# Squared-ReLU attention and a low-rank mixer on one core: the first eight outputs of batch 0 built in another order

## The chip, the cores and the metric

The kernel runs on one core of one Trainium2 chip. The metric is the device time of one execution in microseconds (us). Its engines: PE (TensorE, matmuls; PEld is its weight load), ACT (ScalarE), DVE (VectorE), POOL (GpSimd, which here issues the casting DMAs), SP (SyncE, which here issues the transposing DMAs).

## The reference

```python
# u, v: 8 x 3136 x 256; z: 8 x 3136 x 64; float32
scores = (1.0 / S) * np.matmul(z, z.transpose(0, 2, 1))
attn = np.maximum(scores, 0.0) ** 2
x = u * np.matmul(attn, v)
# U: 3136 x 32, V: 32 x 3136, w_ch1: 256 x 1024, w_ch2: 1024 x 256
h = x.transpose(0, 2, 1) @ U @ V
m = x + h.transpose(0, 2, 1)
out = m + np.maximum(m @ w_ch1, 0.0) @ w_ch2
```

Scores are symmetric in the two positions. The inputs have no bias and no mask.

## The kernel before, in words

The 3136 rows are 24 full tiles of 128 and a tail of 64, 25 in all (NT), of which tile 24 (NF) holds the tail twice over two halves of partitions. A *block* (o, j) is the 128x128 piece of attn that joins output tile o to tile j of v. By symmetry only about half of the blocks are computed: the *panel* `A[j]` holds the 13 blocks (j+k, j), k from 0 to 12, indices modulo 25. `score` (L272) makes pieces of panels: two matmuls on two halves of the array into one tile `ps2` of two PSUM banks (`pair_psum`; there are two such tiles), a ReLU with scale on ACT (L291), a square on DVE (L293). `score_steps` (L295) cuts a panel into two pieces of 832 columns. The other blocks of an output o are those of `A[o]` transposed: `turn` (L311) has SP issue one transposing DMA of 12 blocks into a *strip* (five buffers).

An output's accumulation (`half`, L351) is 49 matmuls, each block against v in two halves of 64 rows that run side by side. Two neighbouring outputs share two PSUM banks (`sets`, two of them); `close_pair` (L360) copies and adds the halves and multiplies by u. The main loop goes over the outputs in the order 12, 13, ..., 24, 0, ..., 11 and has as filler the scores that later outputs need, by hand-written tables (`first_at`, `own_at`, `next_at`). From batch 1 on, the mixer of the batch before (`rank`, `mix`, `low_rank`, and the two channel matmuls L520 and L562, in *bursts*) runs between the outputs.

The engines' order is the program's own. Each engine has one queue, and so have the DMAs of POOL and of SP: an instruction that waits holds those behind it.

Batch 0 has no earlier batch in which its scores could be made ahead. So `start_up` (L607) makes its first eight outputs in two groups of four:

- z comes by POOL DMAs that cast to bf16 (`load_z`, L174), is doubled to 128 columns on DVE (`double_z`, L188), and turned on PE against a unit matrix (`turn_on_pe`, L204), with copies on ACT and DVE (L212).
- Group 1, outputs 12 to 15: for all 25 tiles j the 512 columns of these outputs are scored, in pairs of j. For j from 3 to 11 they are places in `A[j]`; for the other 16 tiles they go to scratch in batch 1's v buffer and in `x_bf`, so that v of batch 1 can only be loaded later. The pair i is scored while the pair i-2 is used. The panels 16 to 19 are made from the middle of this group on, in `nxt`.
- At the border the two pairs close, batch 1's z is doubled (`double_z`) and turned whole by one SP DMA, w2 is fetched (`fetches[3]`).
- Group 2, outputs 16 to 19: stored scores for j from 4 to 15, strips for the rest, with panels 20 to 23 and the rest of panels 8 to 15 (`rest`, 128 to 1024 columns wide) between.

Then the main loop begins with output 20 (i = 8), and loads v of batch 1 in nine pieces at i from 9 to 23.

Of the kernel before, what the change touches and what calls it, by code (L numbers as in the profile page):

```python
# [7 lines left out]
FP32 = mybir.dt.float32  # L8
# [34 lines left out]
def kernel(  # L43
# [11 lines left out]
    nc = tc.nc  # L55
# [136 lines left out]
    def turn_z(b, parts):  # L192
        z_bf = z_tiles[b]
        for t0, t1 in parts:
            transpose(
                out=zT_of(b)[:, t0 : upto(t1), :],
                in_=z_bf[:, t0 : upto(t1), :, :].rearrange("p t h c -> p (t h c)"),
            )
    def turn_on_pe(parts, banks):

        z_bf = z_tiles[0]
        for (t0, t1), ps in zip(parts, banks):
            for t in range(t0, t1):
                mm(  # L204
                    out=ps[:, (t - t0) * P : (t - t0 + 1) * P],
                    lhsT=z_bf[:, t, :, :].rearrange("p h c -> p (h c)"),
                    rhs=eye,
                    start=True,
                    stop=True,
                )  # L210
            copy = nc.vector.tensor_copy if t0 % 8 else nc.scalar.copy
            copy(  # L212
                out=zT_first[:, t0:t1, :].rearrange("p t c -> p (t c)"),
                in_=ps[:, : (t1 - t0) * P],
            )
# [17 lines left out]
    def weight_steps():  # L233
# [21 lines left out]
        def copies():  # L255
# [4 lines left out]
            lambda: wide(w1_bf, moe_w_ch1),  # L260
            narrow,
            fetch,
            lambda: wide(w2_bf, moe_w_ch2),
        ]
        third = FIRST // 2
        puts = [lambda t=t: put(t, t + third) for t in range(0, NF, third)]
# [338 lines left out]
            begun.add((t0, h))  # L605

    def start_up():  # L607
        parts = ((8, 16), (0, 8), (16, NF))
        load_z(0, parts[:2])
        nc.gpsimd.memset(eye, 1.0)  # L610
        nc.gpsimd.affine_select(
            out=eye,
            in_=eye,
            pattern=[[1, P]],
            base=0,
            channel_multiplier=-1,
            compare_op=ALU.is_equal,
            fill=0.0,
        )
        load_v(0, (8, 12))  # L620
        load_v(0, (12, 18))
        load_z(0, parts[2:])
        for part in [(3, 8), (0, 3), (18, NF), (NF, NT)]:
            load_v(0, part)
        double_z(0, parts[:2])
        turn_on_pe([(8, 12), (12, 16)], sets[0])
        turn_on_pe([(0, 4), (4, 8)], sets[1])
        nc.gpsimd.memset(U_bf[:, NF, :], 0.0)
        outs = [FIRST + i for i in range(NG)]
        c0 = FIRST * P  # L630
        for o in outs[::2]:
            open_pair(0, o)
            load_u(0, o)
        if B > 1:
            load_z(1, WHOLE)
        for s in fetches[:3]:
            s()
        nxt = [s for j in range(LEAD, LEAD + NG) for s in turned(0, j)]
        rooms = [v_both[1][:, t : t + 4, :] for t in range(0, NF, 4)]
        rooms = [r.rearrange("p (a t) d -> p a (t d)", a=2) for r in rooms]  # L640
        rooms += [x_bf[:, g].rearrange("p (a w) -> p a w", a=2) for g in (2, 3)]
        pairs = [(8, 9), (10, 11), (12, 13), (14, 15), (6, 7), (3, 4), (5,), (1, 2)]
        pairs += [(0, 16), (17, 18), (19, 20), (21, 22), (23, 24)]
        where = {}

        def make(pair):
            if all(LEAD - 1 - HALF <= j < FIRST for j in pair):
                todo = []
                for j in pair:
                    at = (FIRST - j) * P  # L650
                    where[j] = A[j][:, at : at + NG * P]
                    todo.append((j, c0, NG * P, where[j]))
                score(0, todo)
            else:
                room = rooms.pop(0)
                for i, j in enumerate(pair):
                    where[j] = room[:, i, :]
                score(0, [(j, c0, NG * P, room) for j in pair])

        seen = []  # L660

        def use(pair):
            for j in pair:
                for o in outs:
                    at = (o - FIRST) * P
                    stop = [o % 2 == 1 and len(seen) == NT - 1 - h for h in range(2)]
                    beside(o, j, where[j][:, at : at + P], stop)
                seen.append(j)

        for i, pair in enumerate(pairs):  # L670
            if i == 3:
                double_z(0, parts[2:])
            if i == 5:
                ps = pair_psum()
                turn_on_pe([(16, 20), (20, NF)], [ps[:, 0, :], ps[:, 1, :]])
                turn_on_pe([(NF, NT)], [pair_psum()[:, 0, :]])
                extend_z(0)
            make(pair)
            if i > 5 and i % 2:
                nxt.pop(0)()  # L680
            if i > 1:
                use(pairs[i - 2])
        for pair in pairs[-2:]:
            nxt.pop(0)()
            use(pair)
        for o in outs[1::2]:
            close_pair(0, o)

        outs = [LEAD + i for i in range(NG)]
        for o in outs[::2]:  # L690
            open_pair(0, o)
            load_u(0, o)
        fetches[3]()
        if B > 1:
            double_z(1, WHOLE)
            turn_z(1, WHOLE)
        pairs = [(j, j - 1) for j in range(LEAD - 1, LEAD - FIRST, -2)]

        def use_stored(js):
            for j in js:  # L700
                for o in outs:
                    if 0 <= o - j <= HALF:
                        beside(o, j, block(0, o, j))

        def make_stored(pair):
            todo = []
            for j in pair:
                k0, k1 = LEAD - j, min(NB, LEAD + NG - j)
                todo.append((j, LEAD * P, (k1 - k0) * P, A[j][:, k0 * P : k1 * P]))
            score(0, todo)  # L710

        nxt += [lambda pair=pair: make_stored(pair) for pair in pairs[:2]]
        own = [lambda j=j: use_stored([j]) for j in outs]
        for s in _merge(nxt, own):
            s()
        rest = []
        for j in range(FIRST - NG, LEAD):
            rest += score_steps(0, j, LEAD + NG - j, NB)
        more = [s for j in range(LEAD + NG, LEAD + 2 * NG) for s in score_steps(0, j)]
        for i, pair in enumerate(pairs):  # L720
            if i + 2 < len(pairs):
                make_stored(pairs[i + 2])
            else:
                more.pop(0)()
            use_stored(pair)
            if i == len(pairs) - 1:
                turn(0, LEAD + NG)
        tail = []
        for o in outs:
            js = [(o + 1 + i) % NT for i in range(HALF)]  # L730

            def close(o=o, j=js[-1]):
                beside(o, j, block(0, o, j), [o % 2 == 1] * 2)
                if o % 2:
                    close_pair(0, o)
                if o == outs[1]:
                    load_u(0, LEAD + NG)
                if o < outs[-1]:
                    turn(0, o + NG + 1)

            for i in range(3):
                some = js[4 * i : min(4 * i + 4, HALF - 1)]
                tail.append(lambda o=o, js=some: [beside(o, j, block(0, o, j)) for j in js])
            tail.append(close)
        for s in _merge(tail, more + rest):
            s()

# [3 lines left out]
    for j, i in enumerate((6, 7, 8, 9, 3, 5, 4, 2, 9, 8, 7, 6)):  # L753
        own_at[i].append((j, 0, FIRST - j))

    first_at = {8: [(NT - 1, 0, NB), (0, 0, NB)], 9: [(1, 0, NB)], 10: [(2, 0, NB)]}
    first_at.update({11: [], 12: []})
    for j, i in zip(range(3, FIRST), (9, 10, 11, 11, 11, 12, 12, 12, 12)):
        first_at[i].append((j, 0, FIRST - j))

    next_at = {i: [] for i in range(NT)}
    for j in range(FIRST):
# [12 lines left out]
    for b in range(B):  # L775
# [2 lines left out]
        bursts = bursts_of(b - 1) if b else []  # L778
        burst_at = {4: (0, 1), 8: (2, 3), 13: (4, 5), 17: (6, 7)}
        own = own_at if b else first_at  # L780
        v_at = dict(zip((9, 11, 12, 14, 16, 18, 20, 22, 23), V_PARTS)) if b == 0 else {}
        ahead = dict(zip((2, 3, 6, 7, 10, 11, 14), range(NC)))
        for i in range(begin, NT):
            o = turns(i)
            fill = [s for key in own.get(i, ()) for s in score_steps(b, *key)]
            if more:
# [4 lines left out]
                    turn_z(b + 1, ((FIRST, NF),))  # L791
                if b and i == 10:
                    turn_z(b + 1, ((0, FIRST),))
                if i == 11:
                    extend_z(b + 1)
                if i in v_at:
                    load_v(b + 1, v_at[i])
            main = attend_steps(b, o)
            if b and i in ahead:
                main.insert(17 if (i + (i > FIRST)) % 2 == 0 else 10, lambda c=ahead[i]: low_rank(b - 1, c))  # L800
            _spread(main, fill)
            if i + AHEAD < NT:
                turn(b, turns(i + AHEAD))
            elif more:
                turn(b + 1, turns(i + AHEAD - NT))
            elif i == NT - AHEAD:
                turn_x(b, 0)
            if b == 0 and i in puts:
                puts[i]()
            if b and i == 0:  # L810
# [64 lines left out]
```

## Time and profile before

| what | value |
|---|---|
| four runs, median | 1015.03 us |
| the four | 1013.11, 1025.04, 1014.01, 1016.04 us |
| profiled execution: its own time | 1013.11 us |
| its span, first to last instruction | 1011.4 us |
| TensorE clock granted | 1.00 |
| ACT busy | 613.1 us (61%) |
| DVE busy | 541.3 us (54%) |
| POOL busy | 172.2 us (17%) |
| ReLUs of scores (L291), squares (L293) | 469, 469 |
| strips, issue to landing, median of 196 | 5.3 us |
| u loads of 256 KB, issue to landing, median of 96 | 3.8 us |

How to read it: a group's line gives source line, engine, operation, out<-in, and count; then busy time, mean duration of one, and the idle time of the engine before it with what ended it. In the chain of waits each piece has its start, its length and what it was: work of an engine, or a DMA that something waited for. In a timeline the bracket holds the engine's idle time before and its releaser. A duration is an instruction's own; when like instructions follow one another they overlap, and the spacing is shorter than the duration.

### The profile page before, as it was taken

How to read it: one execution, taken by the hardware profiler on the slowest of the kernel's cores; microseconds unless marked ns; L12 is line 12 of the kernel's file. 1: busy time of each engine (PE TensorE's matmuls, PEld its weight loads, DVE VectorE, ACT ScalarE, POOL GpSimd, SP SyncE). 2: the span in 40 equal slices, each digit the busy share in tenths (PEclk: the TensorE clock that was granted, in tenths of full speed). 3: DMA queues.
4: the chain of work that ended last, by engine and by line, in shares of the span. 5: the costliest groups of instructions: out<-in, count | busy, mean ns of one | idle time of the engine just before them, and what ended most of it. 6: DMA issues, size and time to landing. Idle time of an engine off the chain costs nothing.

```text
span 1011.4 us, 31331 instructions
## 1 busy us (share of the span) xinstructions
PE 988.8 (98%) x13856; PEld 782.3 (77%) x13856; DVE 541.3 (54%) x977; ACT 613.1 (61%) x834; POOL 172.2 (17%) x318
## 2 busy tenths in 40 slices
PE   7799999999999999999999999999999999999998
PEld 5578777787778877788787887878877788777856
DVE  5878654456544664446644556445664356542242
ACT  7877664666645776456764667556674666643154
POOL 4122112121121211121112211112112120011000
PEclk9999999999999999999999999999999999999999
DMA  9999979999898998989989987989979998767432
GB/s 171 148 197 225 179 151 195 179 176 152 163 199 164 177 169 170 166 181 170 159 176 166 183 168 144 193 173 188 156 155 195 170 184 143 144 137 173 101 97 97
DMA packets 414584, 167.70 MB, mean 166 GB/s; under 512 B 389408, under 2 KB 399328, under 8 KB 414448
## 3 DMA queue, kind: packets, MB, share of 16 engines
q1 hardware_dynamic: 384944, 99.16, 60.0%
q0 software_dynamic: 29504, 66.55, 28.0%
q8 instruction: 108, 1.77, 0.7%
q14 instruction: 28, 0.23, 0.1%
HBM read 61.88 MB, written 25.69 MB: 87 GB/s over the span
## 4 chain that ended last, share of the span: by engine, by line
PE 90%; DVE 4%; DMA 3%; ACT 2%; issue 1%; DVEq 0%; ACTq 0%; POOLq 0%
PE ps L351 46%; PE ps L562 17%; PE ps L520 17%; PE ps L278 6%; DMA strip<-A 1%; PE ps L385 1%; PE ps L442 1%; DVE A L293 1%; DVE x_bf L502 1%; ACT A L291 1%; PE ps L488 1%; DMA zT<-z_bf 1%; DVE both L366 1%; DVE x_bf L375 0%; ACT v L291 0%
## 5 line engine op out<-in xcount | busy, mean ns | idle before, releaser
L291 ACT ACTIVATE A<-ps 128x832 bf16<-128x832 f32 (+8 forms) x469 | 352.4, 763 | 155.9 <-PE ps L278 147.1
L351 PE MATMUL ps<-v,A 64*128 64x256 bf16 x4864 | 333.3, 269 | 4.9 <-DVE A L293 2.8
L293 DVE TENSOR_TENSOR A<-A 128x832 bf16<-128x832 bf16 (+8 forms) x469 | 240.5, 524 | 147.3 <-ACT A L291 143.5
L351 PE MATMUL ps<-v,strip 64*128 64x256 bf16 x4420 | 307.3, 269 | 2.5 <-DMA strip<-A 2.5
L351 PEld LDWEIGHTS <-A 64*128 64x128 bf16 x4864 | 238.5, 94 | 48.4 <-issue 13.1
L538 ACT ACTIVATE relu_bf<-ps 128x1024 bf16<-128x1024 f32 (+2 forms) x208 | 187.7, 908 | 142.3 <-PE ps L520 140.3
L351 PEld LDWEIGHTS <-strip 64*128 64x128 bf16 x4420 | 221.7, 94 | 37.2 <-DMA strip<-A 3.0
L562 PE MATMUL ps<-w_bf,relu_bf 128*128 128x256 bf16 x1600 | 204.8, 273 | 0.2 <-ACT relu_bf L536 0.2
L573 DVE TENSOR_TENSOR o_sb<-ps,x_bf 128x512 f32<-128x512 f32 (+1 forms) x104 | 69.7, 670 | 247.4 <-PE ps L562 231.9
L520 PE MATMUL ps<-ut,w_bf 128*128 128x512 bf16 (+2 forms) x896 | 199.4, 353 | 0.3 <-ACT relu_bf L538 0.3
L562 PEld LDWEIGHTS <-relu_bf 128*128 128x128 bf16 x1600 | 155.9, 98 | 47.3 <-issue 3.2
L335 POOL DMA_DIRECT2D u_sb<-in_u_dram x96 | 53.6, 559 | 468.5 <-DVE x_bf L375 435.5
L520 PEld LDWEIGHTS <-w_bf 128*128 128x128 bf16 x896 | 85.0, 98 | 61.1 <-issue 7.0
L278 PE MATMUL ps<-zT 64*128 64x416 bf16 (+8 forms) x812 | 130.7, 312 | 0.0
L365 ACT COPY both<-ps 128x512 f32<-128x512 f32 (+1 forms) x104 | 58.8, 567 | 73.1 <-PE ps L351 65.4
L581 POOL DMA_DIRECT2D out_dram<-o_sb x84 | 46.0, 548 | 270.8 <-DVE o_sb L573 266.8
L366 DVE TENSOR_TENSOR both<-ps,both 128x512 f32<-128x512 f32 (+1 forms) x104 | 69.3, 666 | 27.3 <-ACT both L365 26.9
L375 DVE TENSOR_TENSOR x_bf<-both,u_sb 128x512 bf16<-128x512 f32 (+1 forms) x104 | 69.8, 671 | 3.6
L502 DVE TENSOR_TENSOR x_bf<-ps,x_bf 128x512 bf16<-128x512 f32 (+1 forms) x112 | 65.4, 626 | 8.1 <-PE ps L488 8.0
L278 PEld LDWEIGHTS <-zT 64*128 64x128 bf16 x812 | 42.2, 94 | 4.0
L225 POOL DMA_DIRECT2D v<-in_v_dram x61 | 34.4, 567 | 0.2 <-PE ps L520 0.2
L278 PE MATMUL ps<-relu_bf 64*128 64x416 bf16 (+9 forms) x121 | 23.1, 339 | 2.4 <-ACT A L291 1.3
(52 smaller groups left out, 230.2 us busy)
## 6 DMA issues: line engine op xcount, KB each, us to landing
u_sb<-in_u_dram POOLq DMA_DIRECT2D x96, 256.0 KB, 3.8
out_dram<-o_sb POOLq DMA_DIRECT2D x84, 256.0 KB, 3.0
v<-in_v_dram POOLq DMA_DIRECT2D x57, 192.0 KB, 4.3
strip<-A SPq DMA_TRANSPOSE x196, 5.3
out_dram<-o_sb SPq DMA_DIRECT2D x12, 256.0 KB, 2.1
z_c<-in_z_dram POOLq DMA_DIRECT2D x7, 384.0 KB, 6.3
w_bf<-in_moe_w_ch_dram POOLq DMA_DIRECT2D x2, 512.0 KB, 8.0
u_sb<-in_u_dram POOLq DMA_DIRECT2D x16, 64.0 KB, 2.7
```

Source lines behind the costliest of these rows:

```text
L278: mm(out=ps[:, k, :n], lhsT=zT[halves[k], j, :], rhs=zT_flat[halves[k], c : c + n], start=True, stop=True,)
L291: nc.scalar.activation(out=dst, in_=src, func=AF.Relu, scale=sc)
L293: nc.vector.tensor_tensor(out=dst, in0=dst, in1=dst, op=ALU.mult)
L351: mm(out=acc[t0][h][:, (o - t0) * D : (o - t0 + 1) * D], lhsT=w[halves[h]], rhs=v_both[b % 2][halves[h], j, :], start=start, stop=stop, **kw,)
L365: nc.scalar.copy(out=both[:, :w], in_=banks[1][:, :w])
L366: nc.vector.tensor_tensor(out=both[:, :w], in0=banks[0][:, :w], in1=both[:, :w], op=ALU.add)
L375: nc.vector.tensor_tensor(out=x_at(b, t0, n), in0=split(both[:, :w]), in1=u_sb[:, :n, :].rearrange("p t (a c) -> p t a c", c=P), op=ALU.mult,)
L502: nc.vector.tensor_tensor(out=q, in0=split(ps[h][:, : len(ks) * D]), in1=q, op=ALU.add)
L520: mm(out=ps[i][:, :w] if apart else ps[:, i, :w], lhsT=w1_bf[:, db, (hp + i) * P : (hp + i + 1) * P], rhs=uT[c][:, db, len(chunks[c]) * P ...
L538: nc.scalar.activation(out=relus[c][:, hp : hp + 2, :w], in_=ps[:, :, :w], func=AF.Relu)
L562: mm(out=ps[:, k * D : (k + 1) * D], lhsT=relus[c][:, ht, q : q + P], rhs=w2_bf[:, ht, :], start=(ht == 0), stop=(ht == NH - 1),)
L573: nc.vector.tensor_tensor(out=o_sb[:p, :nk, :].rearrange("p t (a c) -> p t a c", c=P), in0=split(ps[:p, : nk * D]), in1=x_at(b, t, nk)[:p] ...
```

## The change

- z's first two parts come as fp32 by SP DMAs into the two u buffers; DVE writes one copy to bf16, ACT the other (`first_z`). Seven matmuls on zeros run before. The part 16 to 24 of z is loaded and doubled as before, at an earlier place in POOL's queue, and turned before the third step.
- Group 1 makes no scratch scores. Stored scores stay, now for j from 0 to 11 as far as they lie in panels; the panels 12 to 15 are made whole, then 16 and 17. The blocks of outputs 12 to 15 on the other side of the diagonal are turned on PE against the unit matrix, 48 of them, into a `ps2` tile and copied into strips (`mirror`): two copies of 1024 columns on DVE, two of 1024 and four of 512 on ACT.
- v of batch 1: seven of nine pieces are issued by POOL right behind the fetches of w1, U and V; the last two at i = 13 and 17. A small SP read (`mark`) of the seventh piece stands in SP's queue before the first strip.
- Group 2 makes panels 18 to 22; panels 23 and 24 go to i = 8 and 9 of the main loop with their turns. Batch 1's z is doubled and turned in two parts inside group 2.
- w2 is fetched in two halves in batch 1, at i = 0 and 2.

```diff
+    def first_z(parts):
+        z_bf = z_tiles[0] = stage.tile([P, NT, 2, dqk], BF16, name="z_bf")
+        wide = zT_rest[:, :4, :].rearrange("p t c -> p (t c)")
+        nc.vector.memset(wide, 0.0)
+        ps = pair_psum()
+        for _ in range(7):
+            mm(out=ps[:, 0, :], lhsT=zT_rest[:, 0, :], rhs=wide, start=True, stop=True)
+        landed = []
+        for t0, t1 in parts:
+            z_f = u_pool.tile([P, 2, D], FP32, name="u_sb").rearrange("p a c -> p (a c)")
...
+            nc.sync.dma_start(out=z_f, in_=rows(z[0])[:, t0:t1, :])
...
+        for (t0, t1), z_f in zip(parts, landed):
+            nc.vector.tensor_copy(out=z_bf[:, t0:t1, 0, :], in_=z_f)
+            nc.scalar.copy(out=z_bf[:, t0:t1, 1, :], in_=z_f)
...
-            copy = nc.vector.tensor_copy if t0 % 8 else nc.scalar.copy
+            copy = nc.vector.tensor_copy if t0 % 8 and t1 < NF else nc.scalar.copy
...
-            lambda: wide(w2_bf, moe_w_ch2),
+            lambda: wide(w2_bf[:, NH // 2 :, :], moe_w_ch2[H // 2 :, :]),
+            lambda: wide(w2_bf[:, : NH // 2, :], moe_w_ch2[: H // 2, :]),
...
     def start_up():
-        parts = ((8, 16), (0, 8), (16, NF))
-        load_z(0, parts[:2])
+        first_z(((8, 16), (0, 8)))
...
+        load_z(0, ((16, NF),))
+        for part in [(8, 12), (12, 18), (3, 8), (18, NF), (0, 3), (NF, NT)]:
             load_v(0, part)
...
+        run(fetches[:3])
+        if B > 1:
+            for part in V_PARTS[:7]:
+                load_v(1, part)
+        turn_on_pe([(8, 12), (12, 16)], sets[0])
+        turn_on_pe([(0, 4), (4, 8)], sets[1])
+        double_z(0, ((16, NF),))
...
+        def mirror(copy, *blocks):
+            def make():
+                flat = pair_psum().rearrange("p a w -> p (a w)")
+                c = 0
+                for o, m0, m1 in blocks:
+                    for m in range(m0, m1):
+                        mm(
+                            out=flat[:, c + (m - m0) * P : c + (m - m0 + 1) * P],
+                            lhsT=A[o][:, (m + 1) * P : (m + 2) * P],
+                            rhs=eye,
...
+                    copy(
+                        out=strips[0, o][:, m0:m1, :].rearrange("p m c -> p (m c)"),
+                        in_=flat[:, c : c + n],
+                    )
...
+        steps = [
+            stored((8, 9), first), stored((10, 11), first),
+            panel(12, 0), panel(12, 1), stored((6, 7), first),
+            panel(13, 0), panel(13, 1), stored((3, 4), first),
+            mirror(by_dve, (12, 0, 8)), panel(14, 0),
+            mirror(by_act, (13, 0, 8)), panel(14, 1),
+            stored((5, 2), first), stored((1, 0), first), panel(15, 0),
+            mirror(by_act, (12, 8, 12), (13, 8, 12)), panel(15, 1),
+            mirror(by_dve, (14, 0, 8)), panel(16, 0),
+            mirror(by_act, (15, 0, 8)), panel(16, 1),
+            mirror(by_act, (14, 8, 12), (15, 8, 12)),
+            panel(17, 0), panel(17, 1),
+        ]
+        for n, (make, uses) in enumerate(steps):
+            if n == 2:
+                turn_on_pe([(16, 20), (20, NF), (NF, NT)], [*sets[1], sets[0][0]])
+            if n == 4:
+                extend_z(0)
+            if n == 18 and B > 1:
+                nc.sync.dma_start(out=mark, in_=v_both[1][:1, V_PARTS[6][1] - 1, :8])
+            make()
+            if n > 1:
+                av(steps[n - 2][1], ends)
...
+        todo = [stored(js, LEAD) for js in ((11, 10), (9, 8), (7, 6), (5, 4))]
+        rest = [s for j in range(8, FIRST) for s in score_steps(0, j, LEAD + NG - j, NB)]
+        steps = [
+            (panel(18, 0)[0], []),
+            (panel(18, 1)[0], [(o, j) for j in sides for o in low]),
+            (panel(19, 0)[0], [(o, j) for j in sides for o in high]),
+            (panel(19, 1)[0], own[16] + own[17]),
+            (todo[0][0], []),
+            (todo[1][0], own[18] + own[19]),
+            (todo[2][0], todo[0][1]),
+            (todo[3][0], todo[1][1]),
+            (panel(20, 0)[0], todo[2][1]),
+            (panel(20, 1)[0], todo[3][1]),
+        ]
+        for k, s in enumerate(rest):
+            steps.append((s, mirrored[16][3 * k : 3 * k + 3]))
+        for k in range(4):
+            steps.append((panel(21 + k // 2, k % 2)[0], mirrored[17][3 * k : 3 * k + 3]))
+        for o in high:
+            steps.append((None, mirrored[o]))
...
+            if B > 1 and n in (10, 12):
+                part = ((0, FIRST), (FIRST, NF))[n // 2 - 5]
+                double_z(1, (part,))
+                turn_z(1, (part,))
...
-    first_at = {8: [(NT - 1, 0, NB), (0, 0, NB)], 9: [(1, 0, NB)], 10: [(2, 0, NB)]}
+    first_at = {8: [(NT - 2, 0, NB)], 9: [(NT - 1, 0, NB)], 10: [], 11: [], 12: []}
+    first_turns = {8: (NT - 2,), 9: (NT - 1, 0)}
...
-        v_at = dict(zip((9, 11, 12, 14, 16, 18, 20, 22, 23), V_PARTS)) if b == 0 else {}
+        v_at = dict(zip((13, 17), V_PARTS[7:]))
...
+            if b == 1 and i in (0, 2):
+                fetches.pop()()
```

`av(uses, ends)` issues the accumulating matmuls of the listed blocks (o, j) and closes a pair behind its last one. `uses` of a step are the blocks that it makes ready; in group 1 they are accumulated two steps later, in group 2 those listed beside a step follow it at once.

## The prediction, made before the changed kernel ran

> **What bounds the kernel now.** I read the shares on the page first, then a table of windows, then the chain of waits in order of time up to 75 us, then the timeline of the same stretch.
>
> ```profile
> PE 988.8 (98%) x13856; PEld 782.3 (77%) x13856; DVE 541.3 (54%) x977; ACT 613.1 (61%) x834; POOL 172.2 (17%) x318
> ```
>
> TensorE is busy for 98% of the span. The windows say where the other 2% lies (columns: length, then busy time and instructions of PE, PEld, DVE, ACT, POOL, then clock, DMA share, GB/s):
>
> ```profile
> 0.00:60.00 60.00, 44.40 (x637) 34.37 (x639) 41.87 (x82) 46.85 (x72) 16.04 (x34) 1.00 1.02 166
> 60.00:1011.40 951.40, 944.38 (x13223) 747.97 (x13217) 499.45 (x896) 566.29 (x763) 156.11 (x284) 1.00 0.88 166
> 7.50:49.00 41.50, 33.66 (x486) 25.76 (x485) 32.33 (x64) 35.87 (x57) 8.78 (x16) 1.00 1.07 176
> 49.00:60.00 11.00, 8.29 (x139) 6.70 (x135) 7.17 (x14) 8.53 (x13) 1.07 (x2) 1.00 1.12 184
> ```
>
> In the first 60 us PE idles 60.00 - 44.40 = 15.6 us; in the other 951 us, 7.0. The change rewrites the first 49 us, so what it can win lies in those 15.6: about 5 before the first turn, 7.8 while ACT is busy for 35.87 of 41.5 us (86%), and 2.7 from 49 to 60. The chain names the waits:
>
> ```profile
> 1.30 3.04 DMA z_c<-in_z_dram
> 4.36 0.65 DVE z_bf L188 x2
> 5.06 1.89 PE ps L204 x16
> 7.53 2.06 ACT A L291 x4
> 9.59 0.93 ACT v L291
> 17.75 0.76 ACT A L291
> 29.71 1.87 DVE z_bf L188 x2
> 46.23 9.23 DMA strip<-A
> ```
>
> z's load, then ScalarE, then the doubling of z for batch 1 (1.87 us on DVE, at the border between the two groups of four), then a strip that waits for the SP queue. In the timeline:
>
> ```profile
> 13.34 0.44 PE L204 MATMUL ps<-eye,z_bf 128*128 128x128 bf16 x5 [0.67 <-ACT relu_bf L212]
> 31.61 8.56 SPq L195 DMA_TRANSPOSE zT<-z_bf  x1
> 51.11 0.72 PE L351 MATMUL ps<-v,A 64*128 64x256 bf16 x10 [1.19 <-DVE A L293]
> 55.51 0.28 PE L351 MATMUL ps<-v,strip 64*128 64x256 bf16 x1 [1.52 <-DMA strip<-A]
> ```
>
> One transpose of all of batch 1's z holds the SP queue for 8.56 us, and strips queue behind it: PE pays 1.52 us at 55.5, and 1.19 at 51.1 for a late square. The loop from output 20 on begins at 48.9 us.
>
> **The change, part by part.** Unit prices on ACT are spacings in runs of the same kind: 0.515 us for 128x512 (four in 2.06), 0.93 for 128x1024, 0.76 for 128x832; for 384, 256 and 128 columns the single durations 0.53, 0.43, 0.36 less the 0.1 by which a 512 alone (0.61) exceeds its spacing; a plain copy of 512 is 0.585.
>
> *First z.* Before, z lands at 4.33 and the first score starts at 6.88. After, SP loads it. The nearest row is SP's store of 256 KB, 2.0 us to landing (most 3.7); the POOL load took 3.0. From 0.75 that is 2.8 to 4.5; I take 3.4, the second part 0.6 later. Doubling: one copy on DVE (0.34 to 0.69) beside one on ACT (0.585), so 4.0 and 4.6. Sixteen turns at 0.09 (0.44 for five) follow, to 5.8; the first score starts at 5.85, its activation at 6.3 instead of 7.53. Gain 1.2 us, between 0 and 2. The seven matmuls on zeros lie in PE's 5 idle us and cost nothing unless they run past 4.0.
>
> *ScalarE's list up to output 20.* Before: scratch scores 8 x 0.93 = 7.44, panels 16 to 22 14 x 0.76 = 10.6, upper blocks 128 to 1024 wide 4.5, stored scores of the first group 9 x 0.515 = 4.64 and of the second 4.64 + 0.95 (384, 256 and 128 wide) = 5.6, tail turn and closes 2.1: 34.9, and the window measured 35.87. After, first group: stored 4.64 + 0.95 = 5.6, turn copies 1.43, panels 12 to 17 12 x 0.76 = 9.1, mirrored copies 2 x 0.93 + 4 x 0.585 = 4.2, a close 0.6: 20.9. Second group: panels 18 to 22 7.6, stored 5 x 0.515 + 0.95 = 3.5, rest 1.5, a close 0.6: 13.2. Together 34.1. So the scratch goes, but full panels and copies take its place: ACT saves under 1 us.
>
> *PE's list.* Score columns fall by 6912, two matmuls at a time: 3456 columns, at 0.22 us for 512, 1.5 us less. The 48 turns add 48 x 0.09 = 4.3 (bounds: half that if weight loads hide, 48 x 0.279, a turn's own duration, if nothing overlaps). PE is not the bound here, so they cost only where ACT waits.
>
> *Where the loop begins.* At ACT's share of before, 34.1 / 0.864 = 39.5 us from 6.3 is 45.8; then 24 uses of strips with no ACT work, 24 x 0.109 = 2.6 (16 matmuls in 0.87): 48.4. Bounds: ACT never waiting, 6.3 + 34.1 + 2.6 = 43.0. From above, a walk through the steps by hand: two score tiles, so a step's matmuls wait until the step two before is read out. ACT then waits 0.6 for the bank of the tail turn, 1.5 at the first mirrored block (DVE's copy of 1024 from PSUM, twice its 0.69 for 512, holds the tile), 0.9 at the third, 0.4 at several others; the first group ends at 32.0 and the loop begins at 49.3, or 50.7 if the tail of z lands at 8 and not 6.5 and holds DVE's queue, where the squares stand behind it. I take 48.4, 0.5 before today's 48.9: it rests on this stretch's own measured share.
>
> *Moved behind the loop's begin.* Panel 23, two halves, PE-bound there: 2 x 0.175 = 0.35 more.
>
> *Batch 1's z.* Doubled in two parts inside the second group, where PE uses strips and needs no square at once, and turned in halves. Halves on SP later in this trace take 1.9 to issue and 4.4 to land (median of 12), not 8.56 and 12.1. Two from 42.5 leave SP at 46.5; strip 21 lands at about 51 and is needed at the end of output 20, about 52. Output 20's blocks are all squared before. So both waits of 49 to 60 go: -2.7; 0 of it if strip 21 is 3 us late.
>
> *Loads.* Nine v pieces stood in POOL's queue behind u loads from 53 to 98 us; seven now stand behind V's fetch and ahead of the u loads of outputs 16 and 18, which are needed at 40 or later. POOL needs 0.55 each, 3.9 us, hidden. The new small SP read waits for the seventh, with strips 16 and 17 behind it; strip 16 is used from 41. Five v pieces, 1536 KB, landed between 3.04 and 15.0, 128 KB/us; seven make 1344 KB, 10.5 us, from about 23 (V landed at 24 before): 33.5, and strip 16 (3.7 to 5.5 to land) by 39: hidden. w2's halves are issued near 108 and 116 behind u's waits; at w2's own 6.8 to 9.2 us to land the second is there by 125, and the first down matmul stands at 127.25: hidden by 2 us, else it costs what is missing.
>
> A single turn in this trace has a mean duration of 279 ns, and yet five came in 0.44 us, 0.09 apart; the sum goes by the spacing. A rule of the Trainium skill speaks against this change: *TensorE: Matmul & The Clock Gate*, Part 4 (PE-mode transpose), gives about 275 ns for a 128x128 turn in a kernel's context; taken as a rate, 48 turns would be an estimated 13.2 us of PE, 8.9 more than in the sum.
>
> **Sum.** -0.5 + 0.35 - 2.7 = -2.85 on the profiled execution's 1013.1 (span 1011.4 and 1.7 around it): 1010.3. Of the four runs (median 1015.03) one, 1025.04, stands 9 us apart; the middle of the other three is 1014.0, 0.9 above the profiled one. So 1011.2.
>
> **Rivals.**
> - *ScalarE never waits.* For it: ACT had 86% already, and the new order has no border between the groups. Against: two score tiles, shared with mirrored blocks that DVE empties. The loop begins at 43.0: 5.4 less than in the sum, 1005.8.
> - *The small SP read is late: slower than before.* If the v pieces land as slowly as w2's 512 KB did (9.2 us), seven take 24, from 23 to 47; strip 16 lands at 52, PE waits 11 at 41: 1011.2 + 11 = 1022. It decides from the point where the read ends after 36. For it: DMA share 1.0 to 1.2 in this stretch. Against: v's own rate, and strips and w2 no longer run beside it.
> - *Turning costs what it saves.* The walk's 50.7 and strip 21 still late: +2.3 and +2.7: 1016. For it: DVE's PSUM copies and PE's turns stand in the same two tiles. Against: no border wait is left.
> - *Nothing of what it says is felt*: v and w2 loads cost PE no wait in the trace of before, so if the rest balances out the time is that of before, 1014.0; the sum already holds 0 for them.
>
> **How the numbers follow.** The likeliest (0.5) gives 1009 to 1014, number 1011.2. ScalarE never waiting 0.17 (1005 to 1008); turning costs what it saves 0.2 (1014 to 1018); the SP read or w2 late 0.1 (1016 to 1025); the rest, a start that gains nothing or a transfer that stalls later, 0.03. From 1005 to 1018 leaves out about 0.12. A measurement can tell about 1% (10 us) from no change. Faster by that needs 10 of the 15.6 idle us, 5 of which are the first load: 0.04. Slower by that needs the second rival at its worst: 0.05. Within 1%: 0.91.
>
> **What would show it.** Right: first score activation near 6.3; ACT busy 85 to 90% from there to the first matmul of output 20, at 47 to 49.5; no wait for a strip before 60; PE idle in the first 60 us 7 to 9 (15.6 less 2.85 less the 2.8 us of added work, less the 3 us of matmuls on zeros); the SP read over by 36; no wait at the first down matmul. Wrong: ACT waiting for PE or for a score tile at each mirrored block (loop past 50.5); the read past 36 and PE waiting for strip 16; turns spaced 0.2 us or more; loop begun before 45.

## The result, and the profile after

| what | before | after |
|---|---|---|
| median (runs) | 1016.23 us (56) | 1018.82 us (35) |
| lowest to highest | 1011.65 to 1036.77 | 1013.68 to 1026.03 |
| ratio to before, 95% interval | | 1.0022 [1.0007, 1.0037] |
| profiled execution, its span | 1013.11, 1011.4 us | 1024.6, 1022.9 us |

The change made the kernel 0.2% slower, where 0.3% faster was predicted: 1018.82 us against 1011.2. Runs of one kernel spread over more than 1%, and the two profiled executions stand on opposite sides of their medians, so their distance of 11.5 us is not the change's size; the trace shows where time goes, the ratio how much on average.

The changed kernel's lines: L207 matmuls on zeros, L223 and L231 turns of z and their copies, L298 scores, L311 ReLU, L333 strips, L195 batch 1's z, L371 accumulation, L385 and L391 a pair's close, L685 and L698 mirrored blocks and their copies, L753 the small SP read. Windows of the changed kernel, in the columns of the table before (busy time of PE, PEld, DVE, ACT, POOL, then clock, DMA share, GB/s):

```profile
0.00:60.00 60.00, 43.48 (x605) 32.99 (x607) 35.19 (x72) 42.35 (x68) 17.14 (x37) 0.97 1.06 170
60.00:1022.90 962.90, 952.88 (x13301) 757.47 (x13297) 501.88 (x902) 570.53 (x770) 153.80 (x280) 1.00 0.89 164
6.30:47.40 41.10, 34.82 (x518) 27.43 (x518) 29.30 (x62) 34.91 (x58) 10.58 (x21) 1.00 1.09 182
47.40:60.00 12.60, 3.96 (x66) 3.27 (x62) 3.50 (x6) 3.85 (x5) 1.07 (x2) 0.84 1.15 151
```

The stretch that the change rewrites is in order: from the first score to the loop's begin, ACT is busy for 34.91 of 41.1 us, 85%. But in the 12.6 us behind it PE works for 3.96. The chain of waits, some of its pieces:

```profile
1.26 3.17 PE ps L207 x7
4.43 0.68 PE ps L223 x8
6.31 1.35 ACT A L311 x3
...
38.58 7.57 DMA strip<-A
...
48.87 10.81 DMA strip<-A
...
73.76 8.41 DMA strip<-A
```

The front is as meant: z turned from 4.43, the first score activation at 6.31. Then three strips, two of them with waits of PE of over 2 us behind them. PE's timeline from the loop's begin:

```profile
47.41 0.70 PE L371 MATMUL ps<-v,A 64*128 64x256 bf16 x8
...
50.49 0.59 PE L371 MATMUL ps<-v,strip 64*128 64x256 bf16 x5
59.72 0.39 PE L371 MATMUL ps<-v,strip 64*128 64x256 bf16 x1 [8.64 <-DMA strip<-A]
...
82.80 0.35 PE L298 MATMUL ps<-zT 64*128 64x416 bf16 x2 [2.08 <-ACT A L311]
```

Output 20's first matmul starts at 47.41, 1.6 us sooner than before (48.98). Then one strip costs 8.64 us where the trace of before had 1.19, for a late square, and 1.52, for a strip. SP's timeline says which one:

```profile
30.21 0.80 SPq L753 DMA_DIRECT2D mark<-v  x1
31.06 13.09 SPq L333 DMA_TRANSPOSE strip<-A  x5
44.25 4.44 SPq L195 DMA_TRANSPOSE zT<-z_bf  x2
48.87 8.55 SPq L333 DMA_TRANSPOSE strip<-A  x2
```

Strips 16 to 20, the two halves of batch 1's z, then strip 21, issued at 48.87 and landing 10.81 us later. PE asks for a block of it at 51.1, in output 20's last step.

The first mixer matmul of batch 0 stands at 118.97 us, before at 107.94: 11.0 of the 11.5 us between the two spans are lost by then, and from there each batch takes 122.2 to 123.4 us, the last 111.1, in both kernels. Of these 11.0: the loop's begin -1.6, panel 23 +0.35 as priced, the wait for strip 21 +5.9 (8.64 less 2.71), waits between 73 and 83 +2.6 (0.54 and 2.08, none of them before), and PE work at half the clock in 59.7 to 62.8 and 83.3 to 86.7, half of which is lost, +3.2. That makes 10.5.

### The profile page after: what moved, and what is told of

The parts are those of the page before. It is cut to its first block, busy times and chain, and to the rows that moved or that the text cites. A ratio compares the mean times of both kernels' runs of the same rounds, so it can differ in the third digit from the quotient of the medians.

```text
span 1022.9 us, 31437 instructions
## 1 busy us (share of the span) xinstructions
PE 996.4 (97%) x13902; PEld 790.5 (77%) x13902; DVE 537.1 (53%) x974; ACT 612.9 (60%) x838; POOL 170.9 (17%) x317
## 4 chain that ended last, share of the span: by engine, by line
PE 89%; DMA 4%; DVE 4%; ACT 3%; issue 0%; ACTq 0%
PE ps L371 45%; PE ps L582 17%; PE ps L540 16%; PE ps L298 6%; DMA strip<-A 3%; ACT A L311 2%; PE ps L462 1%; DVE x_bf L522 1%; DVE A L313 1%; PE ps L405 1%; DMA zT<-z_bf 1%; PE ps L508 1%; DMA ut<-x_bf 1%; DVE both L386 1%; DVE x_bf L395 0%
## 5 line engine op out<-in xcount | busy, mean ns | idle before, releaser
L311 ACT ACTIVATE A<-ps 128x832 bf16<-128x832 f32 (+9 forms) x472 | 353.7, 761 | 166.1 <-PE ps L298 153.4
L371 PE MATMUL ps<-v,A 64*128 64x256 bf16 x4896 | 338.0, 271 | 0.3 <-ACT relu_bf L231 0.3
L313 DVE TENSOR_TENSOR A<-A 128x832 bf16<-128x832 bf16 (+9 forms) x472 | 241.1, 523 | 164.6 <-ACT A L311 161.3
L371 PE MATMUL ps<-v,strip 64*128 64x256 bf16 x4512 | 313.5, 269 | 9.4 <-DMA strip<-A 9.4
L371 PEld LDWEIGHTS <-A 64*128 64x128 bf16 x4896 | 243.7, 94 | 42.9 <-issue 11.2
L371 PEld LDWEIGHTS <-strip 64*128 64x128 bf16 x4512 | 228.0, 94 | 43.6 <-DMA strip<-A 10.2
L298 PE MATMUL ps<-zT 64*128 64x416 bf16 (+8 forms) x812 | 131.5, 313 | 2.1 <-ACT A L311 2.1
L385 ACT COPY both<-ps 128x512 f32<-128x512 f32 (+1 forms) x104 | 58.9, 566 | 76.1 <-PE ps L371 67.4
L386 DVE TENSOR_TENSOR both<-ps,both 128x512 f32<-128x512 f32 (+1 forms) x104 | 69.2, 666 | 28.6 <-ACT both L385 28.3
L298 PEld LDWEIGHTS <-zT 64*128 64x128 bf16 x812 | 42.9, 94 | 6.0 <-issue 2.3
L298 PE MATMUL ps<-relu_bf 64*128 64x416 bf16 (+10 forms) x112 | 21.1, 323 | 4.1 <-ACT A L311 2.4
```

Source lines behind the costliest of these rows:

```text
L298: mm(out=ps[:, k, :n], lhsT=zT[halves[k], j, :], rhs=zT_flat[halves[k], c : c + n], start=True, stop=True,)
L311: nc.scalar.activation(out=dst, in_=src, func=AF.Relu, scale=sc)
L313: nc.vector.tensor_tensor(out=dst, in0=dst, in1=dst, op=ALU.mult)
L371: mm(out=acc[t0][h][:, (o - t0) * D : (o - t0 + 1) * D], lhsT=w[halves[h]], rhs=v_both[b % 2][halves[h], j, :], start=start, stop=stop, **kw,)
L385: nc.scalar.copy(out=both[:, :w], in_=banks[1][:, :w])
L386: nc.vector.tensor_tensor(out=both[:, :w], in0=banks[0][:, :w], in1=both[:, :w], op=ALU.add)
```

## The experiments

My first theory was that batch 1's z stands in SP's queue ahead of strip 21 and takes its lead. Its rivals: the u loads of outputs 16 to 20, the small SP read, or v of batch 1 slow the strips down. All diffs are against the changed kernel unless the text says otherwise, and most runs have 12 timed executions. "Ratio" is to the kernel before, with its 95% interval. In the recorded expectations e1 and e2 are the first two experiments here, e13 and e14 the two in which batch 1's z is turned sooner; the *lead* of a strip is the time from its issue to its first use.

**Batch 1's z turned later**, in the main loop: the first half behind strip 23, the second behind strips 24 and 0.

```diff
                 double_z(1, (part,))
-                turn_z(1, (part,))
...
+            if b == 0 and i in (8, 9):
+                turn_z(1, (((0, FIRST), (FIRST, NF))[i - 8],))
```

> Changed kernel, but the two transposes of batch 1's z are issued behind strip 23 and behind strips 24 and 0 instead of ahead of strips 21 and 22. Theory Q (SP's queue of transposes is the bound between 31 and 62 us, about 3 us for each of twelve blocks, and PE waits for strip 21 because two halves of z stand before it): strip 21 lands 5 to 8 us earlier than in the changed kernel (59.6 in its profile), PE's wait of 8.6 us at 51 falls to 0 to 3, TensorE's clock stays at 1.00, and the time falls by 4 to 8 us against the changed kernel (ratio to before about 0.996). Theory U (u loads beside the transposes slow them, the order does not matter): strip 21 gains 3 at most, the wait is 5 or more, ratio 1.000 or above.

1015.72 us, ratio 0.9995 [0.9964, 1.0025], above the 0.996 that was expected. The wait near 50 is gone: strip 21 is issued at 44.13 and lands at 47.86. In 50 to 60 PE is busy throughout, against 1.36 us in the changed kernel (first row this run, second row, in a fence of its own, the changed kernel):

```profile
50.00:60.00 10.00, 10.00 (x174) 9.36 (x172) 6.82 (x14) 8.27 (x12) 1.04 (x2) 1.00 1.25 187
```

```profile
50.00:60.00 10.00, 1.36 (x22) 0.94 (x18) 1.88 (x4) 1.60 (x3) 0.54 (x1) 0.80 1.20 143
```

A wait of 1.75 us is left at 68, for strip 1, and ACT waits there too. ACT's timeline:

```profile
69.79 0.38 ACT L311 ACTIVATE A<-ps 128x256 bf16<-128x256 f32 x1 [4.17 <-DMA strip<-A]
```

ACT may not write batch 1's scores into a panel of which batch 0's strip is still being made. The same wait stands at 82.26 in the changed kernel (4.32 us). The prediction did not look at it.

**The u loads moved away**: those of outputs 16 to 19 ahead of v into other buffers, that of output 20 to group 2's start.

```diff
+        for o in (LEAD, LEAD + 2):
+            load_u(0, o, out_pool, "o_sb")
...
-            load_u(0, o)
+        load_u(0, LEAD + NG)
...
-            if n == len(steps) - 3:
-                load_u(0, LEAD + NG)
```

> Changed kernel, order of transposes kept, but u of outputs 16 to 19 is loaded ahead of batch 1's v pieces (into the output buffers, idle in batch 0), and u of outputs 20 and 21 behind those pieces; so no u load is issued between about 34 and 52 us. Theory U: the packets of a transpose take 20 to 29 ns and not 47 to 62, strip 21 lands before 53, PE's wait at 51 is 0 to 2 us, ratio to before about 0.996. Theory Q: strip 21 stays 5 us or more late, ratio 1.000 to 1.003.

1018.76 us, ratio 1.0012 [0.9983, 1.0041]. PE still waits 3.79 us for strip 21, between what the two theories expected. So these loads are not what puts strip 21 behind its use. That they lengthen the wait is possible, not shown: variants that keep them have waits of 2.01 to 8.64 us.

**Both moves together.**

> The changed kernel with the moves of e1 and of e2 together. If both theories hold in part, PE waits nowhere for a strip before 70 us, the loop's output 20 begins near 47.4 as in the changed kernel, and the time is 4 to 6 us under that of before (ratio 0.994 to 0.996), which is the sum that was predicted. If neither holds, it stays at 1.000 to 1.003.

1016.74 us, ratio 1.0024 [0.9998, 1.0049]: no wait near 50 again, and 2.38 us at 71.5. It is 1.0 us above the first experiment by the median and 2.9 by the ratio, and the intervals overlap; the 0.994 to 0.996 expected is not reached. Inconclusive on the sum, clear on the wait.

**The small SP read left out.**

```diff
-                nc.sync.dma_start(out=mark, in_=v_both[1][:1, V_PARTS[6][1] - 1, :8])
```

> Changed kernel without the small SP read of batch 1's v that stands before the first strip. In the changed kernel's profile that read is issued at 30.2 and strip 16 at 31.1, and panel 16 is not squared before about 30: theories Q and U both say no change, 0.998 to 1.002 against the changed kernel. Rival M (the read holds the strips back): strip 16 is issued 2 us or more earlier and the wait at 51 falls by as much.

1018.04 us, ratio 1.0018 [0.9988, 1.0047]; strip 21 is issued at 47.90 and PE waits 3.21 us. The read is not the cause.

**v of batch 1 loaded in the main loop** as before, and no small read.

```diff
-            for part in V_PARTS[:7]:
-                load_v(1, part)
...
-        v_at = dict(zip((13, 17), V_PARTS[7:]))
+        v_at = dict(zip((9, 11, 12, 14, 16, 18, 20, 22, 23), V_PARTS)) if b == 0 else {}
```

> Changed kernel with batch 1's v loaded in nine pieces in the main loop, as in the kernel before, and without the small SP read. Theory Q: v was not what PE waited for, early or late; strip 21 is as late as in the changed kernel without the read (PE waits 3 us at 50), and pieces beside the strips of 53 to 98 us cost 0 to 3 us more: ratio to before 1.001 to 1.005. Rival V (the early v pieces slow the start): the loop begins 1 us or more earlier than 47 and the time falls below the changed kernel's.

1020.73 us, ratio 1.0031 [1.0002, 1.006]; waits of 2.01 us at 50.4 and 3.52 at 59. Early v is not the cause.

**In the kernel before, batch 1's z turned in halves in the main loop**: the same edit as the first experiment's, with the whole turn at the border taken away.

> Kernel before with one edit: the transpose of batch 1's z leaves the border of the two groups and is issued in two halves in the main loop, behind strips 24 and 0. Theory Q (the place in SP's queue decides): strips 18 to 21 no longer stand behind it, the wait of 1.5 us for a strip at 54 goes and the one of 1.0 at 44 too; 1 to 2.5 us less than before, ratio 0.998. If the order of the queue does not matter, both waits stay and the ratio is 1.000.

1019.4 us, ratio 1.0012 [0.9981, 1.0043]. No strip wait, but now z's second half is late:

```profile
71.25 0.21 PE L278 MATMUL ps<-zT 64*128 64x64 bf16 x2 [2.79 <-DMA zT<-z_bf]
```

So z's place does not help in every order.

**Strips and halves one output further ahead**: panel 1 at i = 9, strips 1 to 4 issued an output sooner, z's halves at i = 8 and 10.

```diff
-    first_turns = {8: (NT - 2,), 9: (NT - 1, 0)}
+    first_turns = {8: (NT - 2,), 9: (NT - 1, 0, 1), 10: (2,), 11: (3,), 12: (4,)}
...
+            if b == 0 and i in (8, 10):
+                turn_z(1, (((0, FIRST), (FIRST, NF))[i // 2 - 4],))
```

> Changed kernel with the halves of batch 1's z behind strip 23 and behind strip 2, and with panel 1 scored one output earlier, so that strips 1 to 4 are issued one output earlier than in the changed kernel. e1 had a wait of 1.75 us at 68 left, and ScalarE waited 4 to 5 us to write a panel that a strip's transpose was still reading. Theory Q: both go, PE waits for no strip before 106 us, the mixer of batch 0 begins at 104 to 105 us (107.9 before, 106.2 in e1), ratio to before 0.996. Rival: the loop is bound by transposes as such, then the wait only moves, and the ratio stays at 0.999 to 1.002.

1022.4 us, ratio 1.0051 [1.0025, 1.0078]. This test failed by its own doing: z's second half, at i = 10, was begun by SP only at 65.19, behind strip 2, and was wanted at 65.8.

```profile
72.42 0.24 PE L298 MATMUL ps<-zT 64*128 64x64 bf16 x2 [6.58 <-DMA zT<-z_bf]
```

**DVE's two mirrored copies given to ACT** (`by_dve` to `by_act` for outputs 12 and 14).

> Changed kernel with the two mirrored copies that DVE made given to ScalarE, so that ScalarE makes all. By the walk of the prediction DVE's copy of 1024 columns (2 x 0.69) holds a score tile and ScalarE waits 1.5 us there: the wait goes, but ScalarE has 1.9 us more to do, so the second close of group two comes within 1 us of 47.7. If ScalarE is the bound outright, it comes 1.9 us later.

One execution, 1015.76 us. The second group's second close starts at 46.1, in the changed kernel at 47.7 and in the other variants whose first pair closes by 25.2 at 46.6 to 48.3. So ScalarE, given more work, is not later, and the wait for the strip is still 2.46. One execution does not tell a gain of 1 us.

Up to here a second theory was open: that SP's transposes are simply too many between 31 us, where the small read lets them begin, and 51, and that z is only the last of them.

**Strips 16 and 17 turned on PE**, so that SP has two transposes less; z's halves stay in group 2.

```diff
+                if part and j in (16, 17):
+                    strips[0, j] = strip_pool.tile([P, HALF, P], BF16, name="strip")
...
+            (mirror(by_dve, (16, 0, 8))[0], []),
+            (mirror(by_act, (17, 0, 8))[0], []),
+            (mirror(by_act, (16, 8, 12), (17, 8, 12))[0], []),
```

> Changed kernel with strips 16 and 17 also turned on PE, in the second group (24 turns more, one copy of 1024 columns on DVE, one on ScalarE, two of 512 on ScalarE), so that SP's transposes begin with strip 18. Theory Q2 (transposing on the DMA engines is the bound from where SP starts, 31 us, until the backlog is gone near 70; a strip costs 2.5 to 3 us of it): two strips less, so strip 21 lands 4 to 6 us earlier in respect of the loop; the loop begins 1.5 to 2.5 us later, PE's wait at 50 is 0 to 1, time 0 to 3 us under the changed kernel's, ratio to before 0.999 to 1.002. If the wait has another cause than the backlog (the u loads, the place of z), it stays at 3 us or more and the ratio goes to 1.004.

1023.32 us, ratio 1.0062 [1.0032, 1.0093]. SP has nothing to issue from 39.8 to 45.9 us, and still:

```profile
59.51 0.39 PE L371 MATMUL ps<-v,strip 64*128 64x256 bf16 x1 [4.32 <-DMA strip<-A]
```

SP's timeline of this run:

```profile
48.55 3.39 SPq L195 DMA_TRANSPOSE zT<-z_bf  x2
52.05 3.25 SPq L333 DMA_TRANSPOSE strip<-A  x1
```

The second theory falls: with room in the queue, strip 21 is again late by what stands directly before it, and it takes 7.4 us from its issue to its landing. The turns on PE cost more than they give (group 2's second close starts at 51.8, in the changed kernel's two profiles at 47.7 and 48.3).

**z late and only strip 16 on PE.**

> e1 (halves of batch 1's z behind strips 23 and 0) with strip 16 also turned on PE. Q2: the backlog that was left in e1 (a wait of 1.75 us at 68, ScalarE's wait of 4 for strip 1) is shorter by one strip; loop begins 1 us later than in e1, the mixer of batch 0 begins at 105.5 to 106.5 us (106.2 in e1), ratio to before 0.998 to 1.000. If the waits of e1 are not of the backlog, both stay and the time is 1 us over e1.

1020.26 us, ratio 1.0035 [1.0003, 1.0067]; no strip wait near 50, waits of 2.41 and 2.02 for ACT in 73 to 81.

**In the kernel before, a small SP read at the border ahead of strips 16 and 17.**

```diff
+            nc.sync.dma_start(out=mark, in_=z_tiles[1][:1, 0, 0, :8])
+            turn(0, LEAD)
+            turn(0, LEAD + 1)
             turn_z(1, WHOLE)
```

> Kernel before with one edit: a small SP read of batch 1's doubled z stands ahead of strip 16, so that SP starts its transposes at about 31.6 us as in the changed kernel, and not at 21.75. Nothing else moves. Q2: strips 16 and 17 are done by 36 to 38 and not 30, the whole queue shifts, PE's waits for strips from 38 to 60 grow from 2.5 to 5 to 8 us, ratio to before 1.003 to 1.006. If the start of SP does not matter, the waits stay at 2.5 and the ratio at 1.000.

1021.01 us, ratio 1.0037 [1.0004, 1.007]. Strip 16 is issued at 33.5 instead of 21.75, and PE waits 1.01 and 3.06 us for strips at 41 and 47. That is 4.07 us in all, where the profile before had 0.97 and 1.52, and short of the 5 to 8 expected. A later begin of the strips costs the kernel before as well, which fits the lead of each strip as what counts.

**z of batch 0 loaded as before**, without the matmuls on zeros.

> Changed kernel with the first two parts of z loaded and doubled as in the kernel before (POOL load, four DVE copies), without the seven matmuls on zeros. By the prediction's step the first score's activation moves from 6.3 back to about 7.5 us, and the later marks of group one (its first close at 25.0) move by the same 1.2. If the early z buys nothing past the first activation, the close stays at 25.0.

One execution, 1016.76 us. The first pair closes at 27.7 us, and the clock is full only from 13.9 us; in the changed kernel's two profiles it closes at 25.0 and 26.5. So the new way of loading is worth 1 to 3 us at the start; one execution does not tell what of it is left at the end.

**z of batch 1 turned sooner**, in group 1, ahead of all strips.

```diff
+            if B > 1 and n in (14, 16):
+                part = ((0, FIRST), (FIRST, NF))[n // 2 - 7]
+                double_z(1, (part,))
+                turn_z(1, (part,))
             if n == 18 and B > 1:
...
-            if B > 1 and n in (10, 12):
-                part = ((0, FIRST), (FIRST, NF))[n // 2 - 5]
-                double_z(1, (part,))
-                turn_z(1, (part,))
```

> Changed kernel with the doubling and the two transposes of batch 1's z moved from the second group into the first (steps 14 and 16), where SP's queue stands idle until 31 us; they then precede the small SP read. Theory L (lead: strip 21 is made at 44 to 46 us, used at 50 to 51, and needs 4 to 6 us to land, so the two halves of z before it in SP's queue are the whole wait at 50; a wait over about 2 us also halves TensorE's clock for 3.4 us): strip 21 is issued at 44 to 46 and lands by 51, PE waits 0 to 1 us at 50, strips 1 and 2 come 2 to 4 us earlier than in e1 and its wait at 68 goes; the mixer of batch 0 begins at 104 to 106 us; ratio to before 0.995 to 0.998. Against it: if the strips' landing beside u loads is the cause, the wait at 50 stays at 2 or more and the ratio at 1.001 or more.

1014.2 us, ratio 0.9964 [0.9932, 0.9995]: faster than the kernel before, by 0.05 to 0.7%. SP's timeline, and PE's:

```profile
21.94 11.24 SPq L195 DMA_TRANSPOSE zT<-z_bf  x2
33.24 0.81 SPq L757 DMA_DIRECT2D mark<-v  x1
34.10 18.55 SPq L333 DMA_TRANSPOSE strip<-A  x8
```

```profile
47.10 0.70 PE L371 MATMUL ps<-v,A 64*128 64x256 bf16 x8
...
50.18 0.59 PE L371 MATMUL ps<-v,strip 64*128 64x256 bf16 x6
50.51 1.03 PE L371 MATMUL ps<-v,A 64*128 64x256 bf16 x14
...
71.97 0.35 PE L298 MATMUL ps<-zT 64*128 64x416 bf16 x2 [1.95 <-ACT A L311]
```

The halves take 5.5 and 5.7 us each to issue beside v's pieces, but nothing waits for them there. Strips then follow one another: strip 21 is issued at 45.13, lands at 49.02, and PE goes through 50.5 without a gap. The wait near 70, which was expected to go, stays. The profiles alone don't show the gain over the kernel before: the first mixer matmul stands at 108.1 here (104 to 106 expected) and at 107.94 there, in an execution that was 3.1 us under its kernel's median.

**The same with the strips further ahead**, as in the experiment of that name, to take that last wait too.

> e13 with panel 1 scored one output earlier and strips 1 to 4 issued one output earlier. L: whatever wait for strips 1 and 2 or for the writing of panel 1 is left in e13 between 65 and 80 us goes too: 0 to 2 us less than e13. If ScalarE, which makes more scores in output 21 then, is what holds PE there, it is equal or up to 1 us slower.

1020.63 us, ratio 1.0025 [0.9995, 1.0056]; the wait for ACT is 3.67 us at 76.4. A u load and a strip both took over 11 us to land at 67. Why is open.

**The changed kernel once more**, on the chip of the last two.

> The changed kernel as it is, on the same chip as e13 and e14, so that they can be set against it directly. L: a wait of 2 to 8 us for strip 21 near 50 with half clock behind it, a second wait near 75, ratio to before 1.000 to 1.004.

1020.0 us, ratio 1.0028 [0.9998, 1.0058], 5.8 us above the kernel with z sooner, on the same chip. Its strip wait:

```profile
56.74 0.38 PE L371 MATMUL ps<-v,strip 64*128 64x256 bf16 x1 [5.08 <-DMA strip<-A]
```

The second wait expected near 75 is not in this profile: the longest there is 0.54 us, at 70. By the first mixer matmul this profiled run is 4.3 us behind that of z sooner (112.4 against 108.1), of 5.1 between their spans.

## Why the prediction was wrong, point by point

- *First z*: right. First score activation at 6.31 (6.3 predicted). The matmuls on zeros ran past 4.0, to 4.43, but the first turn starts at 4.22, 0.1 behind the last copy of z that it needs.
- *Where the loop begins*: right, and a little better: 47.41, predicted 48.4. Panels, stored scores and mirrored copies keep ACT at 85%, as assumed from its 86% before. ScalarE never waiting and turning costing what it saves, both rivals, are out for this stretch; of the latter only its second half came true, strip 21 still late, at more than its 2.7.
- *Turns on PE*: right. Eight come in 0.57 to 0.62 us, 0.07 to 0.08 each, 0.09 predicted. The Trainium skill, *TensorE: Matmul & The Clock Gate*, Part 4 (PE-mode transpose), gives about 275 ns for one; as a rate it is not what these rows show.
- *Loads*: right. The small read is issued at 30.21 and over by 31.0, strip 16 behind it at 31.06, and PE does not wait for it; w2's second half lands at 131.4 and the first down matmul starts at 138.7 without waiting for it. The rival of a late read is out.
- *Batch 1's z*: this step failed. It said: "So both waits of 49 to 60 go: -2.7; 0 of it if strip 21 is 3 us late." The wait did not go but grew, to 8.64 us in one profiled execution of the changed kernel and 5.08 in the other. Three sizes were wrong, all in one direction. The two halves left SP at 48.7, not 46.5, since SP came to them at 44.25 and not at 42.5, behind five strips that took 13.09 us. Strip 21 needed 10.8 us to land, not 4.5; 7.6 in the other profile. (In all eight profiles with z's halves ahead of it, it took 4.5 to 10.8, in the six with them elsewhere 3.7 to 3.9: the halves cost it landing time as well as its place.) And it is wanted at 51.1 and not 52, since output 20's last step takes its first block. So the term that was put at -2.7 measured +5.9 in the one profile (8.64 less the 2.71) and +2.4 in the other. The bound for the bad case stopped at "0 of it", and so had no loss in it: the range was too short upwards there. PE idles 16.5 us in the first 60, where 7 to 9 was the sign of being right; with z sooner it is 7.5.
- *A price that was missing altogether*: a long wait of PE is followed by 3.4 us at half clock (below). And a second wait at 68 to 83, for panels that strips hold, was not looked for; it is 2.08 us in the one profile of the changed kernel and missing from the other.

That z's place is the cause of the wait near 50 is shown: in all eight profiles of the new order with z's halves in group 2, PE waits 2.0 to 8.6 us for a strip near 50; in all six with the halves elsewhere it waits there for 0.7 us or less. The first experiment moves the transposes alone and leaves z's doubling where it was. What the wait costs the whole time shows best on one chip: 1020.0 us for the changed kernel, 1014.2 with z sooner, and the two ratios' intervals do not meet. In the other five without the wait the ratios are 0.9995 to 1.0051; they have other waits (1.75 to 6.58 us between 66 and 81), and one of them more turns on PE. The 0.9964 with z sooner fits the 0.9972 that -2.85 of 1014.0 would be. That is in part luck: it has a wait of 1.95 us near 70 and 3.4 us at half clock behind it, which the sum does not hold, and its interval reaches from 0.5 to 6.9 us. Before stands 2.2 us higher in 56 runs than the 1014.0 that the four gave; the rest of the 7.6 us between 1011.2 and 1018.82 is the change, predicted at -2.85 and found at +2.59. The sum was built on one good execution: two other profiles with the old start close their first pair at 28.3 and 28.6 us, the one it read at 26.4.

Open: what is left of the wait near 70; why further-ahead strips made things worse; and why in four of these profiles PE stalls again in a later batch, for 1.1 to 3.3 us, each at other places (415 and 436, 420, 666 and 687, 782 us), which is part of the spread of runs.

## What to carry to other kernels

Here a transfer that was moved into a queue took its whole issue time, and more, from the lead of the one behind it. So look for the first use behind it and set landing time at the slowest seen beside the same traffic, not at the median. Put what nobody waits for soon where the queue has slack, ahead of the deadline traffic rather than in it. Bound a wait that may not go away by its growth as well as by zero, and add what a long idle PE costs afterwards.

## What the runs showed of the hardware

*Half clock after a wait.* The changed kernel's granted clock (the column behind POOL's) around both waits, in windows of 3.4 us:

```profile
56.00:59.40 3.40, 0.00 (x0) 0.00 (x0) 0.00 (x0) 0.00 (x0) 0.00 (x0) 0.50 1.08 148
59.40:62.80 3.40, 3.08 (x28) 2.19 (x30) 0.00 (x0) 0.81 (x1) 0.00 (x0) 0.50 0.80 180
62.80:66.20 3.40, 3.40 (x64) 2.95 (x60) 1.92 (x4) 2.31 (x5) 0.00 (x0) 1.00 0.00 0
79.90:83.30 3.40, 1.32 (x24) 1.01 (x20) 0.36 (x1) 1.04 (x2) 0.00 (x0) 1.00 0.71 150
83.30:86.70 3.40, 3.40 (x36) 2.85 (x33) 2.97 (x5) 2.03 (x4) 0.20 (x1) 0.50 1.11 255
```

In 83.3 to 86.7 PE has 36 matmuls and in 62.8 to 66.2, at full clock, 64. Over the profiles of all kernels here, of 22 waits of PE from 1.0 to 1.75 us (behind the first 9 us) one was followed by 3.4 us or more at half clock; of 24 from 1.95 to 8.64 us, 22 were. So a wait of 2 us could cost up to 1.7 us more, half of such a stretch. The two stretches above begin 27.3 us apart, 8 times 3.41. The Trainium skill, *TensorE: Matmul & The Clock Gate*, Part 1, says that activity is judged in free-running windows of 3.4 us, and that an idle one leads to half clock. The distance agrees with it; but a window with 1.32 us of work in it was enough here.

*The clock at the start.* The windows print a clock of 1.00 before the first record of it as well; there the matmuls of 512 columns start 0.43 us apart, later 0.22, so it is a half until that record. With matmuls on zeros the clock is full before 7 us, but in five of 13 such profiles it fell back to a half for 3.4 us between 9 and 13.5 us, and the first pair then closed at 26.5 to 27.1 instead of 24.6 to 25.2 us. Without them it was full from 8.0 in one profile, the one that the prediction read, and from 13.3 to 13.9 in three.

*Transposing DMAs beside other transfers.* Strip 21 took 3.9 us to land in the kernel with z sooner and 10.8 in the changed one, where the second half of z (landed at 55.59) and two u loads were under way. With the u loads moved away and the half of z still there it took 5.8.
